# A fused attention, Fourier mixing and MLP kernel: the first chunk is transposed by TensorE, the first Fourier stage goes group by group, attention's first stores stand ahead of the weights' later loads, and the planner's numbers are set anew

## The chip, the cores and the metric

One core of one Trainium2 chip. The metric is the time of one execution in microseconds (us) of device time; lower is better. Engines: PE (TensorE; its weight loads are PEld), DVE (VectorE), ACT (ScalarE), POOL (GpSimd), and SP, which only issues DMAs.

## The reference

```python
q, k, v: (8, 8, 576, 64) float32; w_ch1: (512, 2048) and w_ch2: (2048, 512) float64
attn = softmax(mask(q @ k.T / 8)) @ v    # heads 0 to 3: the last 32 positions; 4 to 7: every 32nd position
x    = attn with its heads side by side                        # (8, 576, 512)
u    = x + real(fft(fft(x, axis=1), axis=2))
un   = (u - mean) / sqrt(var + 1e-6)                           # over the last axis
out  = u + relu(un @ w_ch1) @ w_ch2                            # (8, 576, 512) float32
```

## The kernel before

The work is one stream in which four stages overlap. **Attention** takes a batch b as four pairs of heads (b, hp); its outputs go through DRAM (`xd[b]`). **The Fourier stage** (`fft_batch`) reads `xd[b]` back: `xa` by a DMA on SP, and the mirrored rows `xb` by four indirect DMAs on POOL (`fft_load`, L891 to L899). It forms E = xa + xb and O = xa - xb (L907), folds columns (the steps called cosa to cosf and sin, on DVE, ACT and POOL), multiplies by tables on PE (the product A, five column groups; then B, three row blocks), and `sums` adds x to give u. For batch 0 this is done in float32 (`products32`, L1041), for the others in split float16. **Norm** (L1152) normalises 128 rows of u and brings them to PE's layout: `un` (float32) is split into a high and a low float16 half (ACT L1176, DVE or POOL L1179), and one DMA transpose on SP (L1181) writes the tile `uT`. **The MLP** takes 18 chunks of 256 rows: `ups` (L1387, 8 steps of 24 matmuls into PSUM `ph`), `hidden` (L1403 to L1406) and `downs` (L1427). Chunks from `FC=15` on use a folded (Strassen-like) form with other weights, built late by `folds`.

**Weights** arrive as float64, in 16 pieces of 512 KB for each matrix, and are turned into float32 by integer tricks on ACT and DVE (L1221 to L1237, steps c1, cl, sg, c2). TensorE sums their squares into a Gram matrix (L1264), from which scales follow (L1283 on); then they are split into float16 halves: `split` for the first matrix (L1303, L1306), `scaled` for the second (L1339, L1342, and a DMA L1344). Pieces 0 to 7 of the first matrix load straight into place, pieces 8 to 11 into the tiles that held batch 0's q and k (both L1209), pieces 12 to 15 and all of the second matrix through other buffers (L1215), each from a list of kinds (`S0`, `S1`: `u`, `f6`, `uT`, `kt`, `qk`, `pt`), and only after batch 0's gather has landed (`need="xb0"`). A first-matrix product needs its quarter of the split weights; chunk 0's first `downs` needs the second matrix's. c2 of piece i of the second matrix needs the split of piece i of the first, whose place it takes.

**What sets the order.** The program's text does not: each piece of work is a generator that yields `op(engine, cost, get=buffers, need=events, ...)`, and a planner (`Order.run`) picks, in its own model of time, the next op of each engine: the earliest to start, and among those within a small window (`WS`, `WV`, ...) the one with the lowest `bias`, its urgency. The instructions are then issued in that order on each engine's queue. Most of the dictionary `P` holds such urgencies: `l0` for batch 0's loads, `a0` its attention, `w0a` pieces 0 to 11 of the first matrix, `w0` pieces 12 to 15, `f0` batch 0's Fourier stage, `p0` chunk 0's norm, `t2` the third row block's sums, `w1` the second matrix, `a1`, `an` + `db` per batch the later attention. An op with `alt` goes to whichever engine comes first in the plan, with a handicap from `P` (`LO0`, `LE0` for batch 0's O and E: 12.4 and 13.0). While a Gram bank is open, the planner fills PE's planned gaps with small matmuls that change nothing (`rest`, L1272), which keeps PE's clock up:

```python
n = int((est - self.free["T"] - 0.3) / 0.11)
```

`LQ=0` means that no weight load is issued by ACT. `big` is a room of two PSUM tiles of two banks each; `u` is a room of 8 slots, of which each Fourier batch takes 4.

## Time and profile before

| what | us |
|---|---|
| three runs | 948.23, 951.56, 952.43 (median 951.56) |
| the profiled execution | 948.67 |
| its span | 946.9 |
| PE busy in the span | 910.9 |
| DVE, ACT, POOL busy | 717.0, 506.2, 343.5 |

The profile is that of one execution; its span begins with the first instruction and ends with the last, and the execution's own time is 1.8 us longer. Times in rows are us from the span's start unless marked ns. "Busy" of PE counts the filling matmuls too.

### The profile page before, as it was taken

The page shows a single profiled execution, that of the slowest core. Times are in us where ns is not written, and L with a number is a line of the kernel's source. Part 1 is how long each engine was busy: PE and PEld are TensorE (multiplying, and loading weights), DVE is VectorE, ACT ScalarE, POOL GpSimd, SP SyncE. Part 2 cuts the span into 40 slices and gives each one's busy share as a digit, 9 for nine tenths or more (in the row PEclk, how much of TensorE's full clock was granted, in tenths as well). Part 3 has the DMA queues.
Part 4 walks back from the last instruction along what each step waited for, and adds up shares of the span by engine and source line. Part 5 has one row for each costly group of instructions (what it writes and reads, how often), then busy time and mean ns, then how long its engine had stood idle before and what let it go on. Part 6 is the DMA issues. An engine that isn't in the chain of part 4 may idle for free.

```text
span 946.9 us, 25320 instructions
## 1 busy us (share of the span) xinstructions
PE 910.9 (96%) x10597; PEld 668.4 (71%) x10599; DVE 717.0 (76%) x1342; ACT 506.2 (53%) x987; POOL 343.5 (36%) x315
## 2 busy tenths in 40 slices
PE   8778999999899999999999999999999999999997
PEld 6656885766666667665766677676666766689996
DVE  5988875678783896747956966697679889788675
ACT  4848874554653655643746564646423444365452
POOL 0240332245353631335325522552246256334000
PEclk9969999999999999999999999999999999999999
DMA  9788485363335635584445524625240102021100
GB/s 320 243 327 276 136 217 164 121 174 56 92 89 132 151 81 107 105 156 102 117 88 169 116 86 100 173 73 145 44 125 1 45 7 56 18 52 24 41 24 24
DMA packets 140371, 108.41 MB, mean 114 GB/s; under 512 B 108256, under 2 KB 118752, under 8 KB 140256
## 3 DMA queue, kind: packets, MB, share of 16 engines
q1 hardware_dynamic: 137696, 98.40, 38.7%
q0 software_dynamic: 2560, 8.39, 3.0%
q8 instruction: 83, 1.36, 0.6%
q14 instruction: 32, 0.26, 0.1%
HBM read 64.26 MB, written 18.89 MB: 88 GB/s over the span
## 4 chain that ended last, share of the span: by engine, by line
PE 77%; DMA 8%; DVE 7%; issue 3%; POOL 2%; ACT 2%; SPq 1%; DVEq 0%; POOLq 0%; ACTq 0%
PE acc L1427 28%; PE ph L1387 27%; PE acc L1714 5%; PE f L1571 2%; PE B L1038 2%; DMA xb<-xd,ridx 2%; DMA q<-in_w 2%; PE A L1015 1%; PE s L484 1%; DVE fold L1481 1%; PE o L515 1%; DMA W<-in_w 1%; DMA vn<-in_vl 1%; PE f_0x L1571 1%; DMA q<-in_qk 1%
## 5 line engine op out<-in xcount | busy, mean ns | idle before, releaser
L1387 PE MATMUL ph<-uT,W 128*128 128x256 f16 x2880 | 329.3, 273 | 1.2 <-DMA uT<-hb 1.2
L1387 PEld LDWEIGHTS <-W 128*128 128x128 f16 x2880 | 277.4, 98 | 42.8 <-DMA uT<-hb 1.4
L1427 PE MATMUL acc<-W,hb 128*128 128x512 f16 x1344 | 302.6, 379 | 1.5 <-DVE ub L1437 1.5
L1406 POOL TENSOR_TENSOR hb<-hf,hb 128x512 f16<-128x512 f32 x112 | 160.7, 1435 | 279.0 <-ACT hb L1404 196.5
L1427 PEld LDWEIGHTS <-hb 128*128 128x128 f16 x1344 | 129.2, 98 | 143.8 <-issue 1.7
L1403 ACT ACTIVATE hf<-ph 128x512 f32<-128x512 f32 x120 | 71.2, 593 | 180.7 <-PE ph L1387 113.1
L1404 ACT ACTIVATE hb<-ph 128x512 f16<-128x512 f32 x112 | 66.2, 591 | 0.0
L1481 DVE TENSOR_TENSOR fold<-fold,W 128x512 f32<-128x512 f32 x64 | 52.4, 847 | 0.3
L1714 PEld LDWEIGHTS <-tail 128*128 128x128 f16 x504 | 48.3, 98 | 5.3
L461 DVE SCALAR_TENSOR_TENSOR kt<-qk,sc,kt 128x576 f16<-128x576 f32 (+1 forms) x40 | 37.7, 982 | 3.3 <-ACT kt L446 3.1
L907 POOL TENSOR_TENSOR O<-xa,xb 128x1536 f32<-128x1536 f32 x8 | 33.5, 4189 | 16.0 <-DMA xb<-xd,ridx 12.4
L1161 POOL TENSOR_TENSOR rstd<-mv,negh 128x1 f32<-128x1 f32 x30 | 21.7, 730 | 44.0 <-DVE mv L1158 39.5
L1571 PEld LDWEIGHTS <-tail 128*128 128x128 f16 x576 | 34.7, 98 | 2.6 <-issue 1.4
L1658 POOL TENSOR_TENSOR hb<-hb 128x256 f32<-128x256 f32 x13 | 12.2, 950 | 65.4 <-DVE hb L1658 64.3
L1714 PE MATMUL acc<-fold,tail 128*128 128x256 f16 x288 | 35.0, 273 | 0.0
L446 ACT ACTIVATE kt<-qk,sc 128x576 f16<-128x576 f32 (+1 forms) x40 | 29.3, 784 | 10.1 <-DVE sc L402 9.0
L1140 ACT ACTIVATE pq<-B,fcm 128x128 f32<-128x128 f32 (+7 forms) x105 | 27.3, 380 | 11.5 <-PE B L1038 6.3
L1684 DVE TENSOR_TENSOR tail<-hb,tail 128x512 f16<-128x512 f32 (+1 forms) x47 | 31.8, 704 | 1.9 <-ACT tail L1681 1.5
L1681 ACT CAST tail<-hb 128x512 f16<-128x512 f32 (+1 forms) x48 | 25.6, 563 | 9.1 <-DVE hb L1658 5.5
L1179 DVE TENSOR_TENSOR unp<-un,unp 128x512 f16<-128x512 f32 x28 | 22.6, 806 | 9.1 <-ACT unp L1176 9.1
L1028 DVE SCALAR_TENSOR_TENSOR AT<-A,AT 128x290 f16<-128x290 f32 (+3 forms) x35 | 15.1, 479 | 18.8 <-ACT AT L1023 17.1
L897 POOL DMA_INDIRECT xb<-xd,ridx x24 | 26.7, 1111 | 7.3 <-issue 6.1
(313 smaller groups left out, 1550.9 us busy)
## 6 DMA issues: line engine op xcount, KB each, us to landing
qk<-in_qk SPq DMA_DIRECT2D x28, 592.0 KB
sa<-in_w SPq DMA_DIRECT2D x19, 512.0 KB
out<-ub SPq DMA_DIRECT2D x32, 256.0 KB
vn<-in_vl SPq DMA_DIRECT2D x10, 432.0 KB
W<-in_w SPq DMA_DIRECT2D x8, 512.0 KB
xd<-xo SPq DMA_DIRECT2D x16, 256.0 KB
xa<-xd SPq DMA_DIRECT2D x8, 512.0 KB
vn<-in_vs SPq DMA_DIRECT2D x10, 384.0 KB
```

The lines of the kernel that those rows point to most:

```text
L446: A.activation(hi, src, AF.Copy, scale=f)
L461: V.scalar_tensor_tensor(out=lo, in0=src, scalar=f, in1=hi, op0=ALU.mult, op1=ALU.subtract)
L907: tt_ = lambda e, o, x, y, op: e.tensor_tensor(out=o, in0=x, in1=y, op=op)
L1387: T.matmul(ph[:, i, :], W1[:, 4 * (f0 // 512) + d, x, f0 % 512 : f0 % 512 + 128], self.uhl[y][:, d, :], start=(n == 0), stop=(n == 11))
L1403: A.activation(hf, ph, AF.Relu, scale=HS)
L1404: A.activation(hh, ph, AF.Relu, scale=HS)
L1406: G.tensor_tensor(out=hl, in0=hf, in1=hh, op=ALU.subtract)
L1427: T.matmul(self.acc[s], (hh, hl)[x][:, i, 128 * s : 128 * s + 128], W2[:, f, 1 - y, :], start=(f == 0 and n == 0), stop=(f == 15 and n == 2))
L1481: on(e).tensor_tensor(out=w, in0=w if x is None else x, in1=y, op=ALU.add if f else ALU.subtract)
L1571: T.matmul(dst[:, 128 * f : 128 * f + 128], w(x, i)[:, 128 * f : 128 * f + 128], u(y, i), start=opens and f == 0 and n == 0, stop=closes a ...
L1684: on(o).tensor_tensor(out=lo, in0=src, in1=hi, op=ALU.subtract)
L1714: T.matmul(dst, hop[:, x, j, 128 * i : 128 * i + 128], w(y, i), start=bank not in opened, stop=q == 3 and z in (6, 5, 3, 4) and i == 1 and ...
```

## The change

Five edits. (1) In `norm`, chunk 0 alone is transposed by four float32 TensorE transposes of `un` into a `big` tile, and ACT and DVE then write the two float16 halves from PSUM straight into `uT`; the DMA transpose is left out for it. (2) In `products32`, each of the five groups of A is an op of its own with its own copy from PSUM, and the first row block of B is cut in two: its first part needs only the first three groups. (3) In `att_first`, each pair's stores are a thread of their own with urgency -40. (4) First-matrix pieces from `OW=8` on are loaded only after the events of all four pairs' stores. (5) Numbers: `E` and `O` of batch 0 get the handicaps -26.3 and -2.9; `w0a` becomes lower than `a0`; the list `S1` uses `u` slots (two per piece) for five pieces in place of one, `uT` for one in place of four, and `kt` for two in place of four; `M1=(0, 10)` turns two pairs of second-matrix pieces into double ones; the rest are small shifts. `LQ` stays 0. The diff, cut:

```diff
@@ -20,16 +20,16 @@
 B, H, S, D = 8, 8, 576, 64
 
 P = dict(
-    SL2=2.667, SLD2=1.764, GL0=2.7, GD=7.0, LAT=2.22, GL=3.1, t2=47.947, l0=-31.68, a0=-20, sq0=-23.456, w0a=-19.97,
-    c=12.731, z=13.906, f0=-24.028, w0=-22.847, s0=-1.359, w1=3.314, s1=-5.983, p0=-26.912, p1=4.962, pn=-4.352,
-    a1=-14.294, f1=-1.92, a2=0.121, f2=8.514, an=8.61, fn=-44.611, db=1.982, up=19.467, dn=25.786, ev=0.684, WS=0.271,
-    WV=0.084, WA=0.048, WG=0.877, WT=0.185, SL=0.0, SLD=0.818, np=3, AL=3.136, SG=2.918, Lcl=-0.367, Lsg=0.875, LQ=0,
-    LO0=12.439, LE0=13.019, Lc20=-1.501, LSD0=-13.8, al=0.0, Lfs=-1.909, Lwl=-2.741, Lul=-9.275, LO=24.795, LE=5.158,
-    Lc2=-1.062, LSD=-13.902, Lsub=1.259, Lsub0=28.179, Lrt=14.582, Lu=5.511, ORD0=(3, 2, 0, 1),
+    SL2=2.667, SLD2=1.764, GL0=2.7, GD=7.0, LAT=2.22, GL=3.1, t2=32.862, l0=-31.68, a0=-20, sq0=-23.456, w0a=-27.697,
+    c=9.163, z=-19.15, f0=-17.605, w0=-24.7, s0=-1.676, w1=3.484, s1=-7.438, p0=-23.68, p1=4.962, pn=-5.318, a1=-14.294,
+    f1=-1.761, a2=0.709, f2=8.514, an=8.61, fn=-44.611, db=2.56, up=19.467, dn=25.786, ev=1.736, WS=0.048, WV=0.084,
+    WA=0.048, WG=0.932, WT=0.185, SL=0.0, SLD=0.818, np=3, AL=3.136, SG=2.918, Lcl=-0.367, Lsg=0.875, LQ=0, LO0=-2.864,
+    LE0=-26.259, Lc20=-1.677, LSD0=-14.257, al=-0.345, Lfs=-1.909, Lwl=-2.733, Lul=-22.823, LO=19.663, LE=5.158,
+    Lc2=-0.996, LSD=-13.902, Lsub=0.551, Lsub0=22.353, Lrt=13.061, Lu=5.511, OW=8, ORD0=(3, 2, 0, 1),
     vo=([], [], [], [0, 1, 2, 3]), S0=('qk', 'qk', 'kt', 'pt'),
-    S1=('uT', 'kt', 'f6', 'uT', 'kt', 'uT', 'f6', 'f6', 'kt', 'pt', 'uT', 'qk', 'u', 'f6', 'kt', 'qk'), M1=(), HB=4,
-    RB=1, UB=8, VS=1, FC=15, tp=-0.006, ts=0.377, fq=-18.063, fh=-13.401, ff=-23.53, pf=5.385, Lfold=79.934, Lus=0.177,
-    Lhl=1.519,
+    S1=('u', 'u', 'f6', 'uT', 'u', 'f6', 'f6', 'f6', 'kt', 'pt', 'u', 'u', 'qk', 'f6', 'kt', 'qk'), M1=(0, 10), HB=4,
+    RB=1, UB=8, VS=1, FC=15, tp=-0.406, ts=0.309, fq=-18.063, fh=-13.174, ff=-23.53, pf=11.989, Lfold=80.705, Lus=0.177,
+    Lhl=1.525,
 )
 ORD0 = P["ORD0"]
 FP32 = {(b, hp) for b in range(3) for hp in range(4)}
@@ -777,6 +777,9 @@
             yield op("V", 1.35 if hp < 2 else 1.5, put="acc" if acc else "big", note=f"out {hp}")
             g = att_out(0, hp, po, 1e-9, None, xos[hp])
             next(g)
+            spawn(stored(hp, g), bias=-40)
+
+        def stored(hp, g):
             yield op("S", 0.8 if hp < 2 else 1.6, n=3 if hp < 2 else 6, sets=f"xd0_{hp}", note=f"xd0 {hp}")
             next(g, None)
 
@@ -1046,13 +1049,14 @@
         last = ta[0:33, 4 * NE : 6 * NE], tb[0:33, 767 : 767 + 2 * NE]
         for gs in ((0, 1), (2,), (3, 4)):
             first, end = gs[0] == 0, gs[-1] == 4
-            yield op("T", 1.4 * len(gs), get="big f6 -fft" if first else "acc" if len(gs) == 1 else "big", need=f"FH{257 if end else 0 if first else 129}_{b} f32 second",
-                     put="f6 f6 f6" if end else "", note=f"A{gs[0]} {b}")
-            if first:
-                AT = f6(f"AT{b}")[:, 0 : 10 * NE].rearrange("p (g k) -> p g k", g=5)
-                ATs = AT.rearrange("p g (k t) -> p g t k", t=2)
-            ps = (psone if len(gs) == 1 else lambda b, n: psbig(n))(b, f"A{b}_{gs[0]}")
             for i, g in enumerate(gs):
+                yield op("T", 2.2, get="" if i else "big f6 -fft" if first else "acc" if len(gs) == 1 else "big", need="" if i else f"FH{257 if end else 0 if first else 129}_{b} f32 second",
+                         put="f6 f6 f6" if end and i else "", note=f"A{g} {b}")
+                if first and i == 0:
+                    AT = f6(f"AT{b}")[:, 0 : 10 * NE].rearrange("p (g k) -> p g k", g=5)
+                    ATs = AT.rearrange("p g (k t) -> p g t k", t=2)
+                if i == 0:
+                    ps = (psone if len(gs) == 1 else lambda b, n: psbig(n))(b, f"A{b}_{gs[0]}")
                 c0, w = GROUPS[g]
                 cs = 0 if g < 3 else 1
                 d0 = 0 if g < 2 else 129 if g == 2 else 257
@@ -1062,8 +1066,7 @@
                     o = ps[0:w, 512 * i + NE * t : 512 * i + NE * t + NE]
                     T.matmul(o, sd[:, t, d0 : d0 + w], ta[:, 2 * NE * cs + NE * t : 2 * NE * cs + NE * t + NE], start=False, stop=(t == 1))
 
-            def evac(gs=gs, ps=ps):
-                for i, g in enumerate(gs):
+                def evac(g=g, i=i, ps=ps, gs=gs):
                     w = GROUPS[g][1]
                     o = op("A", 0.4, put=("acc" if len(gs) == 1 else "big") if i == len(gs) - 1 else "", sets=f"AT{g}_{b}", note=f"AT{g} {b}", alt=dict(V=(0.48, P["LAT"])))
                     yield o
@@ -1073,11 +1076,11 @@
                     else:
                         V.tensor_copy(ATs[0:w, g], src)
 
-            spawn(evac())
+                spawn(evac())
         cols = (0, 257, 4), (2, 256, 4), (1, 256, 2), (2, 256, 2), (1, 256, 2)
         for t in range(3):
             r = 128 if t < 2 else 33
-            yield op("T", 2.74, get="big" + (" u u" if t < 2 else ""), need=" ".join(f"AT{g}_{b}" for g in range(5)), put="f6" if t == 2 else "", note=f"B{t} {b}")
+            yield op("T", 2.74 if t else 1.64, get="big" + (" u u" if t < 2 else ""), need=" ".join(f"AT{g}_{b}" for g in range(5 if t else 3)), put="f6" if t == 2 else "", note=f"B{t} {b}")
             ps = psbig(f"B{b}_{t}")
 
             T.matmul(ps[:, 0:512], zerb, zero.to_broadcast([128, 512]), start=True, stop=False)
@@ -1085,6 +1088,8 @@
             for g, (c0, w) in enumerate(GROUPS):
                 x = AT[0:w, g, 128 * t : 128 * t + r]
                 k0, k1, st = cols[g]
+                if t == 0 and g == 3:
+                    yield op("T", 1.1, need=f"AT3_{b} AT4_{b}", note=f"Bb {b}")
                 if g == 0:
                     T.matmul(ps[0:r, 0:257:4], x, tb[0:w, 0:65], start=False, stop=False)
                     T.matmul(ps[0:r, 260:509:4], x, tb[0:w, 1:64], start=False, stop=False)
@@ -1167,6 +1172,18 @@
         else:
             un = mp.tile([128, 2, 257], F32, tag=tag, name=f"un{nm}", bufs=P["RB"] if tag == "rt" else 1).rearrange("p a b -> p (a b)")[:, 0:DM]
         V.tensor_scalar(un, u, mv[:, 0:1], rstd, op0=ALU.subtract, op1=ALU.mult)
+        if c == 0:
+            yield op("T", 0.6, get="big", put=tag, note=f"uturn {nm}")
+            ps = psbig(f"ut{nm}")[:, 0:DM]
+            for d in range(4):
+                T.transpose(ps[:, 128 * d : 128 * d + 128], un[:, 128 * d : 128 * d + 128], ident)
+            yield op("A", 0.62, note=f"uhi {nm}")
+            ps = ps.rearrange("p (d t) -> p d t", t=128)
+            hi, lo = (uT[:, 4 * x : 4 * x + 4, 128 * s : 128 * s + 128] for x in range(2))
+            A.copy(hi, ps)
+            yield op("V", 0.75, put="big", sets=f"uT{nm}", note=f"ulo {nm}")
+            V.tensor_tensor(out=lo, in0=ps, in1=hi, op=ALU.subtract)
+            return
         yield op("A", 0.62, get=ptag, note=f"uhi {nm}")
         if ptag == "h":
             hs = hfree.pop(0)
@@ -1203,7 +1220,7 @@
             src = list(wpieces(wi))[i + n][0]
             if kind is None:
                 far = i + n < P["LQ"]
-                yield op("A" if far else "S", 0.4 if far else 1.45, dma=1.25 if far else 0.0, lat=1.6, need=f"sc{ORD0[(i - 8) // 2]}" if i >= 8 else "", at=0 if n else None, note=f"ld {wi} {i + n}")
+                yield op("A" if far else "S", 0.4 if far else 1.45, dma=1.25 if far else 0.0, lat=1.6, need=(f"sc{ORD0[(i - 8) // 2]}" if i >= 8 else "") + ("".join(f" xd0_{hp}" for hp in range(4)) if i >= P["OW"] else ""), at=0 if n else None, note=f"ld {wi} {i + n}")
                 if n == 0:
                     stg = stg1(i, m)
                 (nc.scalar if far else nc.sync).dma_start(stg[:, 512 * n : 512 * n + 512], src)
```

## Rows read from the trace of the kernel before

**Rows 1.** The page's part 1: busy us of each engine, share of the span, instructions

```profile
PE 910.9 (96%) x10597; PEld 668.4 (71%) x10599; DVE 717.0 (76%) x1342; ACT 506.2 (53%) x987; POOL 343.5 (36%) x315
```

**Rows 2.** Three stretches: length; busy us of PE, PEld, DVE, ACT, POOL; clock; DMA

```profile
0.00:92.30 92.30, 72.29 (x1028) 57.05 (x1030) 73.11 (x134) 56.94 (x73) 19.00 (x19) 0.87 0.86 292
92.30:136.00 43.70, 43.02 (x601) 37.64 (x602) 36.46 (x80) 36.34 (x54) 13.94 (x12) 1.00 0.61 165
136.00:946.90 810.90, 795.63 (x8970) 573.76 (x8968) 607.39 (x1130) 412.92 (x861) 310.55 (x285) 1.00 0.36 92
```

**Rows 3.** The filling matmuls (line 1272), sum of stretches from 0 to 200 us

```profile
sum 200.00, PE 26.32 PEld 24.59; mean PE 1.32 PEld 1.23
```

**Rows 4.** The chain that ended last: start, us, what held it

```profile
37.98 1.97 DMA xd<-xo
...
45.95 3.89 DMA xb<-xd,ridx
...
87.97 4.31 DMA uT<-hb
```

**Rows 5.** Timeline: start, us, instruction; batch 0's stores and what stands among them

```profile
21.89 7.26 SPq L859 DMA_DIRECT2D xd<-xo  x6
...
29.13 0.76 DVE L842 TENSOR_TENSOR xo<-o,rs 128x576 f32<-128x576 f32 x1
...
29.46 1.58 SPq L1209 DMA_DIRECT2D q<-in_w  x2
...
37.43 1.15 SPq L847 DMA_DIRECT2D xd<-xo  x2
```

**Rows 6.** Timeline: E, O and folds of batch 0

```profile
50.05 1.76 DVE L907 TENSOR_TENSOR E<-xa,xb 128x1536 f32<-128x1536 f32 x1 [1.08 <-DMA xb<-xd,ridx]
50.09 5.00 POOL L907 TENSOR_TENSOR O<-xa,xb 128x1536 f32<-128x1536 f32 x1 [2.75 <-DMA xb<-xd,ridx]
...
51.85 4.05 DVE L907 TENSOR_TENSOR tmp<-E 128x765 f32<-128x765 f32 x1
...
57.21 0.95 DVE L907 TENSOR_TENSOR E<-O 128x765 f32<-128x765 f32 x1
```

**Rows 7.** Line 907's O on POOL, all batches: ns min/median/max, first and last start

```profile
L907 POOL TENSOR_TENSOR O<-xa,xb x8: 3442/4142/5029, 50.1 to 710.3; 128x1536 f32<-128x1536 f32 x8
```

**Rows 8.** PE in stretches of 2 us: busy, granted clock, DMA share, GB/s

```profile
54.00:56.00 2.00, 0.00 (x0) 0.50 0.97 375
...
72.00:74.00 2.00, 2.00 (x51) 0.50 0.23 94
```

**Rows 9.** Timeline: the end of A, its last copy, and the start of B

```profile
68.57 1.33 PE L1063 MATMUL A<-f32a,O 128*128 128x145 f32 x4
...
71.40 0.51 ACT L1072 COPY AT<-A 128x290 f32<-128x290 f32 x1
...
73.97 0.55 PE L1083 MATMUL B<-zero 128*128 128x512 bf16 x1
```

**Rows 10.** Timeline: six earlier TensorE transposes, and chunk 0's second norm

```profile
13.98 0.88 PE L760 MATMUL pT<-ident,pbt 128*128 128x128 f32 x6
...
84.86 0.55 DVE L1169 TENSOR_SCALAR un<-ub,mv,rstd 128x512 f32<-128x512 f32 x1 [0.45 <-POOL rstd L1161]
...
85.44 0.62 ACT L1176 CAST hb<-un 128x512 f16<-128x512 f32 x1 [0.28 <-DVE un L1169]
...
87.26 0.68 DVE L1179 TENSOR_TENSOR hb<-un,hb 128x512 f16<-128x512 f32 x1
```

**Rows 11.** The later weights' loads (ns, first and last start), and chunk 0's first `downs`

```profile
L1215 SPq DMA_DIRECT2D sa<-in_w x19: 327/369/1005, 52.8 to 112.1; - x19
...
136.01 1.46 PE L1427 MATMUL acc<-W,h 128*128 128x512 f16 x6
```

**Rows 12.** The stretch of batch 0's gather and first folds: columns as in rows 2

```profile
46.00:59.00 13.00, 7.34 (x106) 6.08 (x103) 11.64 (x11) 2.29 (x6) 7.90 (x4) 0.80 0.72 236
```

**Rows 13.** Timeline of PE: its longest wait after 100 us, in brackets

```profile
249.23 0.38 PE L1015 MATMUL A<-csin,FH 128*127 128x145 f16 x3 [2.69 <-DVE AT L1028]
```

More of the change, by code (lines that the diff above doesn't have):

```diff
@@ L709, in loads @@
             for i, hp in enumerate(ORD0):
-                yield op("S", 1.5 if i else 2.7, sets=f"q{hp}", at=0, note=f"q {hp}")
+                yield op("S", 1.75 if i else 2.0, sets=f"q{hp}", at=0, note=f"q {hp}")
                 nc.sync.dma_start(q0s[hp][:, 0 : S + KP], a["qk"][0, hp])
@@ L723, in loads @@
                 for z in [ORD0[n] for n in P["vo"][i]]:
-                    yield op("S", 1.25 if z < 2 else 1.0, at=0, sets=f"v{z}", note=f"v {z}")
+                    yield op("S", 1.65, at=0, sets=f"v{z}", note=f"v {z}")
                     nc.sync.dma_start(src0[z], a[f"v0{z}"])
```

## The prediction

> **What bounds the kernel now.** I read the page's first part, then stretches, then the chain that ended last, then the timeline where the chain leaves PE. PE is busy 910.9 of 946.9 us [rows 1], but that alone misleads: it counts matmuls that only fill gaps. So I cut the span where the nature of the work changes [rows 2]. From 136.0 on PE is busy 795.6 of 810.9 us at full clock; the 15.3 us left are the last stores after PE's end and small waits, the longest of them 2.69 us [rows 13]. That stretch is bound by PE's own work, which the change leaves as it is. Between 92.3 and 136.0 PE is busy 43.0 of 43.7 us, but DVE and ACT too stand at 83%: they prepare the second matrix while PE works off chunk 0's eight `ups`, four of chunk 1 (there are four `hb` buffers) and batch 1's attention. Before 92.3 PE idles 20.0 us, and of its 72.3 busy us 26.3 are fill [rows 2, 3]; from 54 to 74 its clock is granted at 0.50, that is 1.2 GHz, after a stretch without a matmul [rows 8]. So nearly all that can be won lies ahead of chunk 0's first `ups` at 92.3, and it counts only as far as PE has real work afterwards.
>
> The chain of the head [rows 4] is: batch 0's last store lands at 39.95; the gather's last piece lands at 49.84; E, folds and A; B; sums and norm; the DMA transpose lands at 92.28; `ups`. A second chain hangs on the same gather: the later weights may load only then, from 52.8 on [rows 11], and chunk 0's first `downs` waits for them until 136.0.
>
> **The change part by part.** *Stores first.* Pair 1's output is ready at 29.13 + 0.76 = 29.89, yet its last store is issued at 37.43 to 38.58: SP first spends 7.26 us on six stores of pair 3 and then issues loads of weights [rows 5]. With every store at -40 and pieces 8 to 11 behind them, three issues after 29.89 end near 31.5, if the earlier pairs' stores are out by then, which the -40 asks for. That is 38.58 - 31.5 = 7 us. It moves two things. The first weight loads now stand behind stores that SP must wait for, so pieces 1 to 7 land later; and pieces 8 to 11 (2 MB) stand ahead of `xa` in SP's queue. At the 375 GB/s of a full stretch [rows 8] 2.1 MB take 5.6 us. The gather takes 49.84 - 37.43 = 12.4 us from the last issue on, mostly POOL's own issues, so those loads fit beside it; I take 1 us off, with bounds 0 and 5.6; the other way, 2 us more are won if the weights that DVE works on ahead of pair 1's output come too late to hold it up. ACT is busy 2.29 of the 13 us from 46 to 59 [rows 12]: that is the cover for the weights' later arithmetic. Without it, they'd hold chunk 0's fifth `ups`, not its first. Gather: **-6** (-9 to -1).
>
> *E to POOL, O to DVE.* The handicaps decide it: 3.45 - 26.3 beats 1.78 for E, 1.78 - 2.9 beats 3.45 for O. Before, DVE's E took 1.76, POOL's O 5.00, and the next fold 4.05, where a fold of that shape takes 0.95 [rows 6]; that fold ended at 55.90, 0.81 after O ended. So one engine held the other up; E, then O's 5.00 - 1.72 = 3.3, then the fold's last 0.8 came in series. If the other order is in series too, the fold that needs E ends after 1.76 + 3.3 + 0.95 = 6.0 us, against 5.85 before. If they don't hold each other up, it ends after POOL's 3.44 to 4.14 [rows 7] and 0.95, 4.4 to 5.1. I take **0**, bounds -1.5 and +0.4, nearest to the rows of this very place. The Trainium skill's page "SBUF — State Buffer", section "Who interferes with whom", says that GpSimd's port pair is DVE's second one and that the loser blocks for the whole instruction; by it the first reading holds and this swap, which puts the tensor needed first on the slower engine, wins nothing. By the medians alone it would have won 0.7 us; both lie in the bounds.
>
> *A and B by groups.* Five groups of A end at 68.57 + 1.33 = 69.90; the last copy ends at 71.91; B starts at 73.97, as Gram and score matmuls were put between [rows 9]. B's first part now needs only three groups, copied long before, and can start at 69.90. The copies of groups 3 and 4 run beside it. Lower bound 0 (other matmuls still go first: the weights' `w0` is now lower than `f0`), upper 4.1; **-3**, near the upper end because no wait is left there. B's matmuls are as many as before; the five separate ops add no instruction.
>
> *The transpose.* From `un`'s end at 85.41 to `ups` at 92.3 is 6.9 us: ACT 0.62, DVE 0.68 after other DVE work, then the DMA's 4.31 [rows 4, 10]. The new way: four transposes at 0.88/6 = 0.15 make 0.6, then ACT 0.62, DVE 0.68 (both read PSUM now; I take the same), and some 0.4 for hand-overs: 2.3. **-4.6** (-5.0 to -2.5, if a `big` tile is late: B's third block holds one of two until its sums). The two DMA transposes also leave SP's queue, where weight loads stood behind them. PE's cost is 1.2 us for both halves, where it idles or fills.
>
> *Other buffers and double pieces.* Two pieces in one go cost less than two alone; by the planner's own costs (0.69 twice against 1.15 for c1, 1.35 twice against 2.5 for sg, 0.7 twice against 1.24 for c2) both pairs together save 1.2 us of ACT and DVE, which I count as nothing of its own. Five pieces in `u` slots instead of one can hold up B when they are late: B's first two blocks need four of the eight slots. *All loads on SP* removes nothing: `LQ` is 0 in both.
>
> **Sum.** Chunk 0's `ups` start 6 + 0 + 3 + 4.6 = 13.6 us earlier, near 79. But PE's 43.0 us of work then have to last until the first `downs`. The second matrix's loads wait for the gather, so they come 6 us earlier, and I give freed queue, buffers and ACT's idle time 2 us more: `downs` at 128. The other 5.6 us of the 13.6 become fill or idle on PE. So **8 us** are left: 948.7 - 8 = 940.7 for an execution like the profiled one; that one lies 2.9 below the median of the runs, so the median goes from 951.6 to **943.5**. What is late next is the second matrix.
>
> **Rivals.** (a) *The second matrix keeps up*: then the whole 13.6 counts, 938. For it: DVE's 4.05 contains 3 us of waiting, and ACT is idle near the gather [rows 6, 12]. Against: DVE at 83% after [rows 2]. (b) *The second matrix does not move*: DVE and ACT have the same sum of work, pieces 1 to 11 arrive later and collide with the folds; then all of it becomes fill, and 0 to 3 us remain: 950. For it: the same 83%. Against: the loads' start is tied to the gather. That `LQ` makes one part of the change empty belongs here: it gives 0. (c) *Slower, by the later urgencies*: `db` spaces the later batches wider (1.98 to 2.56) and the folded chunks' norm is less urgent (5.4 to 12.0). A chunk whose u is late leaves PE dry, as at 249 for 2.69 us [rows 13]. There are six later batches with such a place; if each costs 2.5 us more, 15 are lost, 7 more than won: 958. It decides above 8/6 = 1.3 us a batch. Against: PE idles only 15.3 us in 811 there now, the end included [rows 2], so the old spacing has slack to give.
>
> **How the numbers follow.** Forecast 0.45, (a) 0.17, (b) 0.20, (c) 0.18. A measurement of this kernel tells some 0.5%, 4.8 us, from no change. Forecast and (a) lie below 946.8: faster 0.62; (b) within: same 0.20; (c) beyond 956.3: slower 0.18. Forecast and (a), with the gather's bounds and some 4 us of other waits after 136, reach down to 934; (b) and half of (c) reach up to 956.
>
> **What would show it.** Right: the last `xd` store of batch 0 issued near 31 to 33, the gather landed at 42 to 46, E on POOL, B's zeroing matmul within 2 us of A's end, no DMA transpose before the first `ups`, that one at 77 to 82, and the first `downs` at 126 to 130 with fill or idle before it. Wrong: a gather past 47 (SP blocked behind loads), `ups` waiting on a `big` tile or a `u` slot, `downs` still at 136, or PE's idle after 136 above 20 us.

## The result, and the profile after

The changed kernel is slower by 1%: a median of 958.60 us over 7 runs (955.73 to 962.64), against 950.87 over 7 runs (946.57 to 952.43) of the kernel before; the ratio is 1.0098, with an interval of 1.0074 to 1.0122. The forecast was 8 us faster, and the time lies above its range. The profiled execution took 958.1 us with a span of 956.2, 9.3 more than before.

The page's first part, then the three stretches of [rows 2] with the last one's end moved:

```profile
PE 917.3 (96%) x10623; PEld 674.8 (71%) x10623; DVE 713.0 (75%) x1333; ACT 506.1 (53%) x986; POOL 343.6 (36%) x317
```

```profile
0.00:92.30 92.30, 69.01 (x858) 54.85 (x859) 63.57 (x114) 50.43 (x61) 23.87 (x19) 0.82 0.77 270
92.30:136.00 43.70, 41.26 (x645) 35.22 (x642) 40.09 (x81) 36.28 (x53) 11.74 (x11) 1.00 0.48 143
136.00:956.20 820.20, 806.99 (x9126) 584.74 (x9124) 609.33 (x1139) 419.38 (x874) 307.96 (x287) 1.00 0.37 93
```

Past 136 PE idles 13.2 us, less than the 15.3 of before: the later batches lost nothing. In the first 92.3 us PE's idle time grows from 20.0 to 23.3, DVE does 63.6 us of work instead of 73.1 and ACT 50.4 instead of 56.9 [rows 2]. The head has grown, and it is the two engines of the weights' arithmetic that did less in it. Windows of ten us say when (columns as in rows 2); first the kernel before, then the changed one:

```profile
20.00:30.00 10.00, 8.00 (x147) 7.12 (x148) 8.23 (x13) 8.19 (x9) 0.00 (x0) 1.00 0.98 383
30.00:40.00 10.00, 6.90 (x89) 6.03 (x87) 9.60 (x21) 9.67 (x9) 0.00 (x0) 0.84 0.77 214
```

```profile
20.00:30.00 10.00, 8.84 (x148) 8.05 (x149) 4.71 (x9) 5.47 (x6) 0.00 (x0) 0.83 0.73 202
30.00:40.00 10.00, 5.16 (x84) 4.58 (x81) 4.74 (x12) 4.57 (x4) 4.33 (x4) 1.00 0.84 284
```

From 20 to 40 DVE works 17.8 us before and 9.5 after, ACT 17.9 and 10.0. Some 8 us of arithmetic of each are pushed behind 40, where the folds of batch 0 want the same engines. SP's timeline shows why (start, us, instruction; rows left out are marked), as against [rows 5]:

```profile
15.47 7.87 SPq L862 DMA_DIRECT2D xd<-xo  x12
23.38 0.84 SPq L1226 DMA_DIRECT2D W<-in_w  x2
...
28.26 1.16 SPq L850 DMA_DIRECT2D xd<-xo  x2
29.46 2.85 SPq L1226 DMA_DIRECT2D W<-in_w  x4
32.41 2.46 SPq L1226 DMA_DIRECT2D q<-in_w  x4
34.97 0.40 SPq L896 DMA_DIRECT2D xa<-xd  x1
45.06 0.33 SPq L390 DMA_DIRECT2D f32a<-in_f32a  x1
```

The last store goes out at 28.3 to 29.4, 9 us earlier than in [rows 5]; 7 were forecast. The gather's last piece `xb` has landed by 45.06 (the last row waits for it), 4.8 us earlier than before. But ten of the twelve early weight pieces now stand behind stores that SP has to wait for, and eight of them (4 MB) ahead of `xa`. What that does to the pieces is seen on the engines' timelines. The kernel before (the last of these pieces reaches ACT; the third scale of the first matrix on PE, L359; the last of its split on DVE; the start of A, and of `ups`):

```profile
35.66 1.22 ACT L1221 ACTIVATE q<-q 128x1024 f32<-128x1024 f32 x1 [0.30 <-DMA q<-in_w]
43.68 0.16 PE L359 MATMUL gram<-s1w,oneb 128*128 128x1 bf16 x1 [0.72 <-DVE s1w L1285]
45.25 3.73 DVE L1306 SCALAR_TENSOR_TENSOR W<-W,scl,W 128x1024 f16<-128x1024 f32 x3
57.13 1.20 PE L1060 MATMUL A<-f32a,FD 33*65 33x290 f32 x2 [5.45 <-DVE FD L907]
92.32 8.03 PE L1387 MATMUL ph<-uT,W 128*128 128x256 f16 x72 [1.21 <-DMA uT<-hb]
```

The changed kernel, with E, O and the first fold of batch 0, which [rows 6] show for before (`tmp`, and its last step into `FD`), the start of A, a wait inside it, and `ups`:

```profile
47.96 1.17 ACT L1238 ACTIVATE q<-q 128x1024 f32<-128x1024 f32 x1 [1.74 <-DMA q<-in_w]
49.29 4.52 POOL L910 TENSOR_TENSOR E<-xa,xb 128x1536 f32<-128x1536 f32 x1 [10.62 <-ACT q L1238]
51.56 7.70 DVE L1254 SCALAR_TENSOR_TENSOR W<-q 128x1024 int32<-128x1024 int32 x2 [0.56 <-ACT q L1248]
53.77 4.41 POOL L910 TENSOR_TENSOR O<-xa,xb 128x1536 f32<-128x1536 f32 x1
59.19 0.94 DVE L910 TENSOR_TENSOR tmp<-E 128x765 f32<-128x765 f32 x1
60.89 0.16 PE L359 MATMUL gram<-s1w,oneb 128*128 128x1 bf16 x1 [0.50 <-DVE s1w L1302]
61.13 2.78 PE L1289 MATMUL gram<-oneb,zero 128*128 128x128 bf16 x47
61.72 0.62 DVE L910 TENSOR_TENSOR FD<-tmp 128x192 f32<-128x192 f32 x2
63.84 0.70 PE L1064 MATMUL A<-f32a,FD 33*65 33x290 f32 x2
66.25 6.21 DVE L1323 SCALAR_TENSOR_TENSOR W<-W,scl,W 128x1024 f16<-128x1024 f32 x4
70.04 0.85 PE L1067 MATMUL A<-f32a,E 128*128 128x145 f32 x2 [2.59 <-POOL E L910]
102.67 2.78 PE L1404 MATMUL ph<-uT,W 128*128 128x256 f16 x24
```

The last pair of pieces reaches ACT 12.3 us later and the third scale comes 17.2 us later. Before, all of this work was over at 48.98, 1.1 us before E could start; now it lies among the folds: on DVE the last c2 (L1254) stands ahead of the fold, and the split (L1323) between the folds and A's later groups; on PE the Gram matmuls, the scale and 47 fill matmuls stand ahead of A. A starts 6.7 us later: its first folds are ready at 62.34 instead of 57.30, which is 5.0 of them, and then PE works off the fill until 63.84. E waited for `xa`: its row names ACT's q, but that ended at 49.13, and the load on SP that waits for `xa` to land starts at 49.14. Chunk 0's `ups` start at 102.67, 10.35 later than before (92.32).

### The profile page after: what moved, and what is told of

It reads as the page before. It is cut to its first block, busy times and chain, and to the rows that moved or that the text cites. A ratio compares the mean times of both kernels' runs of the same rounds, so it can differ in the third digit from the quotient of the medians.

```text
span 956.2 us, 25370 instructions
## 1 busy us (share of the span) xinstructions
PE 917.3 (96%) x10623; PEld 674.8 (71%) x10623; DVE 713.0 (75%) x1333; ACT 506.1 (53%) x986; POOL 343.6 (36%) x317
## 4 chain that ended last, share of the span: by engine, by line
PE 80%; DVE 7%; DMA 7%; ACT 3%; issue 2%; SPq 1%; POOL 0%; DVEq 0%; ACTq 0%; POOLq 0%
PE ph L1404 30%; PE acc L1444 29%; PE acc L1731 6%; PE f L1588 3%; PE B L1041 2%; DVE W L1254 2%; DMA W<-in_w 1%; PE A L1018 1%; DMA q<-in_w 1%; PE s L484 1%; PE o L515 1%; PE f_0x L1588 1%; DMA q<-in_qk 1%; PE f_2x L1588 1%; DMA pT<-qk 1%
## 5 line engine op out<-in xcount | busy, mean ns | idle before, releaser
L1423 POOL TENSOR_TENSOR hb<-hf,hb 128x512 f16<-128x512 f32 x112 | 156.7, 1399 | 282.1 <-ACT hb L1421 189.5
L1498 DVE TENSOR_TENSOR fold<-fold,W 128x512 f32<-128x512 f32 x64 | 55.7, 899 | 0.3
L910 POOL TENSOR_TENSOR O<-xa,xb 128x1536 f32<-128x1536 f32 x8 | 33.5, 4186 | 4.8 <-DMA xb<-xd,ridx 4.8
L1675 POOL TENSOR_TENSOR hb<-hb 128x256 f32<-128x256 f32 x12 | 10.5, 882 | 58.3 <-DVE hb L1675 57.1
L1289 PEld LDWEIGHTS <-zero 128*128 128x128 bf16 x386 | 27.9, 112 | 4.7 <-issue 4.0
L1289 PE MATMUL gram<-oneb,zero 128*128 128x128 bf16 x386 | 30.0, 245 | 0.0
```

The costliest lines, as they stand in the source:

```text
L910: tt_ = lambda e, o, x, y, op: e.tensor_tensor(out=o, in0=x, in1=y, op=op)
L1289: T.matmul(idle[-1][:, 0:128], zerb, oneb, start=False, stop=False)
L1423: G.tensor_tensor(out=hl, in0=hf, in1=hh, op=ALU.subtract)
L1498: on(e).tensor_tensor(out=w, in0=w if x is None else x, in1=y, op=ALU.add if f else ALU.subtract)
```

## The experiments

One table for all (us, read from the timeline of one execution each; idle + fill is PE's in the first 100 us; the ratio is to the kernel before, with its interval). Differences of 2 us between two timelines mean little: x12 has the plan of the kernel before and other instructions only in `norm`, and yet its scale and A come 1.8 us later.

| kernel | third scale | A | B | `ups` | first `downs` | idle + fill | ratio |
|---|---|---|---|---|---|---|---|
| before | 43.7 | 57.1 | 74.0 | 92.3 | 136.0 | 46.3 | 1 |
| changed | 60.9 | 63.8 | 80.0 | 102.7 | 134.4 | 54.7 | 1.0098 |
| x1 E, O swapped | 62.7 | 66.8 | 85.1 | 108.1 | 147.0 | 55.4 | 1.0092 (1.0058 to 1.0126) |
| x2 no -40 | 58.2 | 64.8 | 81.2 | 106.0 | 160.7 | 50.1 | 1.0362 (1.0325 to 1.0399) |
| x3 DMA transpose | 60.1 | 63.6 | 79.2 | 104.0 | 144.5 | 55.1 | 1.0171 (1.0127 to 1.0215) |
| x4 before, TensorE transpose | 45.6 | 59.0 | 75.0 | 93.3 | 139.0 | 46.6 | 1.0013 (0.9997 to 1.0030) |
| x5 `xa` ahead, planned anew | 69.3 | 94.6 | 110.1 | 131.9 | 147.4 | 69.3 | 1.0336 (1.0310 to 1.0363) |
| x6 old numbers | 69.7 | 87.0 | 97.5 | 116.6 | 143.3 | 63.9 | 1.0157 (1.0129 to 1.0185) |
| x7 before, groups | 44.7 | 58.2 | 70.7 | 94.1 | 144.7 | 46.6 | 1.0229 (1.0198 to 1.0259) |
| x8 before, groups, `ph` | 45.5 | 59.0 | 71.5 | 95.3 | 148.2 | 45.1 | 1.0208 (1.0175 to 1.0241) |
| x9 held, `xa` ahead | 63.5 | 66.4 | 82.6 | 105.3 | 136.9 | 55.5 | 1.0143 (1.0102 to 1.0183) |
| x10 held, and E on DVE | 60.3 | 63.2 | 79.4 | 104.2 | 135.9 | 52.1 | 1.0134 (1.0096 to 1.0173) |
| x11 held, `ph` | 61.8 | 65.8 | 81.0 | 105.3 | 137.1 | 52.3 | 1.0142 (1.0097 to 1.0187) |
| x12 before held, `ph` | 45.5 | 58.9 | 75.6 | 93.2 | 136.9 | 45.9 | 1.0012 (0.9992 to 1.0032) |
| x13 held, pieces by POOL | 68.3 | 71.3 | 87.5 | 110.2 | 141.9 | 56.5 | 1.0191 (1.0168 to 1.0214) |
| x14 x13, E on DVE, `ph` | 66.6 | 69.6 | 85.8 | 110.3 | 141.9 | 54.4 | 1.0181 (1.0153 to 1.0209) |
| x15 held, 4 pieces out | 63.0 | 66.0 | 82.2 | 106.7 | 138.4 | 53.0 | 1.0140 (1.0117 to 1.0163) |
| x16 x6, `f6` after A | 71.6 | 71.8 | 83.8 | 104.5 | 158.6 | 53.8 | 1.0186 (1.0155 to 1.0216) |
| x17 before held, late scale | 60.1 | 69.3 | 84.6 | 102.8 | 146.9 | 56.5 | 1.0102 (1.0069 to 1.0136) |
| x18 x16, A ahead | 68.8 | 58.2 | 76.3 | 103.0 | 158.0 | 50.3 | 1.0198 (1.0144 to 1.0251) |

**Parts undone or done alone, planned anew.** x1 gave E and O their old handicaps, `LO0=12.439, LE0=13.019`:

> The changed kernel with one edit: the handicaps of batch 0's E and O are those of before (LE0=13.019, LO0=12.439), so E goes to DVE and O to POOL again. Theory E (both on POOL in series, 49.29 to 58.18, held the fold back to 59.19): the fold of E ends some 4 us earlier after the gather, near 55.5 instead of 60.13, and chunk 0's first `ups` at about 98 to 99 instead of 102.67; the time falls by about 4 us, to 954 to 955. Rival Q (the head is held by SP's queue and by weights' work alone): the fold ends earlier but `ups` stay at 102 to 103, and the time stays at 957 to 960.

E went back to DVE, but behind the pieces: it started at 59.1, and `ups` came at 108.1, later than either theory had it. Neither way of placing E and O is worth anything here; the time did not move.

x2 put the stores' urgency back: `spawn(stored(hp, g))` without `bias=-40`.

> The changed kernel with one edit: the four pairs' stores keep the urgency of the values (about -19.8) instead of -40, so the first matrix's eight first loads stand ahead of all stores on SP, as before; pieces 8 to 11 still come after the stores. Theory Q (SP waits for the stores' data with six weight loads behind it, and 4 MB then stand ahead of `xa`): only 2 MB stand ahead of `xa`, E starts some 3 to 5 us earlier than 49.29 even if the last store is issued later than 28.8, `ups` start at 98 to 100, the time is 954 to 956. Rival (the stores' early issue is what helps, and the loads behind it cost nothing): the last store goes out near 36, E starts at 50 or later, and the time is 959 to 962.

Neither came: the last store went out at 33.5, E started at 48.3, and it is some 25 us slower than the changed kernel (0.0264 of 950), and much of that lies far behind the edit (`downs` 26 us later, PE idle 8.2 us between 180 and 260 where it was 2.7). The planner had laid out everything differently.

x3 left the TensorE transpose out of the changed kernel, x4 put it alone into the kernel before (both by the block at `if c == 0` in `norm`):

> The changed kernel without its first edit: chunk 0's norm goes through the float16 tile and the DMA transpose again. If the TensorE transposes are worth the forecast's 4.6 us even here, `ups` start near 106 to 107 and the time rises to 962 to 963. If their gain was lost to the wait for a PSUM tile (98.92, released by the subtraction of attention's scores at 98.78), `ups` start at 102 to 104 and the time stays within 2 us of 958.6.

> The kernel before with one part of the change alone: chunk 0 is transposed by TensorE through a `big` tile. The forecast's step: from un's end to the first `ups` 2.3 us instead of 6.9, `ups` near 88 instead of 92.3, and 2 to 4 us off the time (947 to 949), less what the second matrix holds back. Rival (a `big` tile is late here too, since attention's scores and the third block of B hold both): 5 to 7 us from un to `ups`, time within 1 us of 950.9.

x3 is 0.7% slower, but `ups` only 1.3 us later; `downs` came 10 us later in the new plan. x4 gains nothing: `ups` come 7.4 us after `un`'s end.

x5 moved `xa` ahead by numbers, `f0=-28.5, OW=4`; x6 kept the new code and took all of the old numbers, with `OW=8`; x7 put the groups of A and B alone into the kernel before; x8 added the transpose with its tile from `ph`.

> The changed kernel with two numbers set otherwise (f0 from -17.605 to -28.5, OW from 8 to 4), so that on SP the load of xa stands right behind the last batch-0 store, ahead of the last four W pieces and the four q pieces (4 MB); the planner then also puts O on DVE and leaves E on POOL. Theory Q (the gather stood behind 4 MB on SP, and O on POOL cost 4.2 us more): xa is issued near 30 and lands by 40 to 43, E starts there instead of at 49.3, and chunk 0's first ups come at 92 to 95 instead of 102.7; since PE was idle or filling before it, 7 to 9 us come back: 950 to 952. Rival M (the end of the head is set by the second matrix, whose arithmetic follows the order of the loads and not the gather): ups come earlier, but the first downs stay within 2 us of 134 or later, and the time is 956 to 962.

> The code of the changed kernel with every urgency of the kernel before (all of P but OW, and S1, M1, tp, ts, pf, Lfold and the like): stores first, A and B by groups and the TensorE transpose stay, single pieces instead of double ones. SP then has xa behind five W pieces instead of eight W and four q, E is on DVE and O on POOL as before. Theory U (the new urgencies are what costs): 943 to 951, with ups at 84 to 90 and the first downs by 134. Rival S (the new structure itself makes the loads late, as all of them but one stand behind stores on SP): slower than before still, 954 to 962, with the second matrix's first W scaled later than 130 and the first downs past 136.

> The kernel before with A and B by groups alone. SP's queue and the gather stay as they were (E at 50 to 52). Theory H (what comes off the head's chain comes off the time): B starts within 1 us of A's end, 3 to 4 us earlier, un ends at 81 to 82.5, ups come at 88.5 to 89.5, and the time is 947 to 949. Rival M (the second matrix sets the end of the head): ups as early as that, but the first downs at 135 to 138 and the time 950 to 953.

> The kernel before with A and B by groups and the TensorE transpose of chunk 0, which takes its PSUM tile from the ph buffers (idle until the first ups) instead of from the two big ones; urgencies, stores and loads as before. No wait for a big tile is left: from un's end to ups 2.5 to 4 us instead of 6.9. Theory H: ups at 84 to 86, time 943 to 947. Rival M: ups at 84 to 86, the first downs at 135 to 138, the time 949 to 953.

None of the four came within either theory's range of the time, and all are slower than the changed kernel too. x5 and x6 did what was wanted of the gather (E at 46.5 and 45.3) and yet A came at 94.6 and 87.0. x7 shows two things. B does start 3.2 us earlier, but at the lower clock; windows of x7 (third number from the end: the granted clock) have 0.50, that is 1.2 GHz, from 70 to 76, where the kernel before has 0.92 from 74 to 76 and 1.00 then, and B takes 11.2 us (70.73 to 81.97) instead of 8.6:

```profile
74.00:76.00 2.00, 1.78 (x5) 1.09 (x6) 1.12 (x2) 1.38 (x4) 0.00 (x0) 0.50 1.03 412
180.00:260.00 80.00, 73.30 (x878) 51.50 (x876) 58.31 (x115) 44.53 (x102) 29.93 (x37) 0.94 0.42 105
660.00:760.00 100.00, 95.77 (x960) 65.16 (x958) 66.63 (x118) 40.70 (x84) 36.83 (x34) 0.98 0.29 72
760.00:860.00 100.00, 93.93 (x766) 66.19 (x764) 89.11 (x141) 43.09 (x93) 33.89 (x29) 0.95 0.09 24
```

And an edit of batch 0 alone, in the first 100 us, cost PE idle time at 180 to 260 (77.31 busy before) and past 660 (100.00 and 97.34 busy before in the same two windows). So the time of a variant that is planned anew says little about the part that was edited. From here on the plan was held where that is said: the planner sees what it saw, and single instructions are moved or replaced by hand at their places.

**Parts alone, with the plan held.** x9: the DMA of `xa` issued when the fourth pair's stores are out:

```diff
             next(g, None)
+            xa_now.append(hp)
+            if len(xa_now) == 4:
+                xa_now.append(xa_load(0))
```

x10: also E by `V` and O by `G` for batch 0. x11: the transposes in `pph.tile(...)` instead of `psbig(...)`. x12: the kernel before, in `norm` for chunk 0:

```diff
-            A.copy(unp[:, 0], un)
+            for d in range(4):
+                T.transpose(ps[:, 128 * d : 128 * d + 128], un[:, 128 * d : 128 * d + 128], ident)
+            A.copy(hi, ps)
...
-            nc.sync.dma_start_transpose(uT[:, :, 128 * s : 128 * s + 128], unp.rearrange("p x d -> p (x d)"))
```

> The changed kernel with its plan held: the planner sees what it saw, every engine keeps its order, and only the DMA of xa is issued by hand right behind the last batch-0 store, ahead of the four W and four q pieces. Theory Q (xa behind 4 MB held E up): xa lands before the gather, E starts on POOL at about 45 instead of 49.3; DVE has the two q pieces in its order ahead of the fold, and they land 1 to 1.5 us later than now, so the fold tmp comes at 56 to 57 instead of 59.2 and ups at 100 instead of 102.7: 2 to 3 us, 955 to 957. Rival D (DVE's order, not xa, is what the fold waits for): tmp within 1 us of 59, ups within 1 us of 102.7, 958 to 960.

> As x9, and E and O of batch 0 on the engines of the kernel before (E on DVE at the place in DVE's order that the plan gives, O on POOL), again with the plan held. Theory P (O on POOL behind E cost 4.2 us): O on POOL from about 45 to 50, E on DVE at 51 to 53, the fold tmp at 54 to 56, ups at 98 to 99.5; 3 to 5 us less than the changed kernel, 953 to 956. Rival D: E stands behind the weights on DVE and the fold comes at 57 or later; 956 to 959.

> The changed kernel with its plan held, and the two TensorE transposes written to the ph buffers instead of the big ones. Theory B (the second transpose waited for a big tile, and that ate the 4.6 us): from un's end to ups 3.5 to 5 us instead of 7.8, ups at 98 to 100, time 955 to 957. Rival M (what follows ups has slack, as the second matrix sets the first downs): ups as early, the first downs within 1.5 us of 134.4, the time 957 to 960.

> The kernel before with its plan held, chunk 0's DMA transposes replaced at their places by TensorE transposes into the ph buffers. The term of the sum by itself: un's end to ups 2.5 to 3.5 us instead of 6.9, ups at 88 to 89.5. Theory H (the head's chain counts in full): 946 to 948. Rival M (the second matrix is the bound from there on): the first downs at 135 to 137 still, and 949 to 952.

x9: E starts at 45.43, 3.9 us earlier, as theory Q has it, and the fold comes at 60.64, even 1.4 later, beyond rival D's range too; the time is no better (1.0143). The last pair of pieces, now behind `xa`, reaches ACT at 50.92, 3.0 us later, so x9 alone doesn't tell the two apart; x15 below, without the loads of the last two pairs, has the fold at 60.68 still. DVE of x9:

```profile
46.03 4.48 DVE L1331 SCALAR_TENSOR_TENSOR W<-W,scl,W 128x1024 f16<-128x1024 f32 x1
50.43 4.45 DVE L1262 SCALAR_TENSOR_TENSOR W<-W 128x1024 int32<-128x1024 int32 x1
...
58.37 2.35 DVE L1262 SCALAR_TENSOR_TENSOR W<-q 128x1024 int32<-128x1024 int32 x2
60.64 0.95 DVE L918 TENSOR_TENSOR tmp<-E 128x765 f32<-128x765 f32 x1
```

The pieces' instructions fill DVE's queue up to the fold, and while POOL runs E and O (45.4 to 53.8) two of them take 4.5 us each instead of 1.2. x10 wins 3.2 us of A by giving E back to DVE, but 1.1 of `ups` and nothing that the runs can tell; the fold comes at 58.5, as rival D had it. x11 takes the wait for a `big` tile away, and from `un`'s end to `ups` it is still 7.5 us (97.75 to 105.28), against 7.8. x12 shows why the transpose wins nothing even in the kernel before. Its PE after the second transpose, and the DVE instruction that ends `uT`:

```profile
87.67 0.66 PE L1174 MATMUL ut<-ident,un 128*128 128x128 f32 x4 [1.86 <-DVE un L1169]
88.16 2.79 PE L1283 MATMUL gram<-oneb,zero 128*128 128x128 bf16 x47
89.46 0.68 DVE L1179 TENSOR_TENSOR uT<-ut,uT 128x512 f16<-128x512 f32 x1
90.95 0.60 PE L573 MATMUL s<-mloc,ident 128*128 128x480 bf16 x3
91.48 1.04 PE L580 MATMUL s<-qk 64*64 64x96 f32 x36
92.45 0.86 PE L1275 MATMUL gram<-W 128*128 128x128 bf16 x12
93.16 2.02 PE L1398 MATMUL ph<-uT,W 128*128 128x256 f16 x17
```

`uT` is whole at 90.14, 2.5 us after `un`'s end at 87.61, as the forecast's 2.3 had it. But planned fill, the scores of batch 1 and Gram matmuls stand ahead of `ups` in PE's order, and `ups` start at 93.16; scores and Gram matmuls ran under the DMA before. The fill, 2.8 us, stays only because the plan is held; what `ups` would win without it is not shown.

**What holds A.** The table's third scale and A go together: in the changed kernel and its variants but x5, x6 and x18, A follows the scale by 0.1 to 6.6 us, mostly by 3; in the kernel before and its variants, x17 apart, by 13.4. Part of that is the order alone: the 3 us are the 47 fill matmuls that every held plan of the changed kernel has between the two. A stands behind the first phase of the weights on PE, and its folds behind it on DVE. x13 gave the loads of pieces 2 to 11 to POOL's queue, `nc.gpsimd.dma_start(...)` at the place of pieces 0 and 1; x14 joined x10 and x11 to it; x15 left out the loads of pieces 8 to 11 (`if i < 8:`) in x9; x16 was x6, planned anew, with `need="xb0 AT0_0" if kind == "f6" else "xb0"` for the second matrix's loads.

> The changed kernel with its plan held; the loads of the first matrix's pieces 2 to 11 (5 MB less the first two pieces) are issued by POOL at the place of pieces 0 and 1, so that none stands behind a store on SP, and xa stands right behind the last store. E and O stay on POOL. Theory W (late weight pieces hold the folds and A, as DVE and PE have them ahead in their order): the third scale's matmul on PE comes at 43 to 50 instead of 60.9, the fold tmp at 50 to 55 instead of 59.2, A at 55 to 59 instead of 63.8, ups at 94 to 98 instead of 102.7; 949 to 954. Rival P (POOL's E and O alone hold DVE until they end, whatever the pieces do): tmp at 55 or later, A at 60 or later, 955 to 958.

> As x13, with E of batch 0 on DVE and O on POOL, and chunk 0's transposes in the ph buffers; plan held. Theory W: E at 44 to 47, tmp ends by 52, A at 52 to 56, ups at 90 to 94, and as PE has work until the first downs near 130 to 134 the time is 944 to 950. Rival M (the second matrix is then the bound): ups as early, the first downs at 133 to 136 with more fill or idle before it, 950 to 955.

> As x9 (plan held, xa right behind the last store), and the loads of pieces 8 to 11 (2 MB) are left out; their arithmetic runs on what lies in the buffers, so the weights are not those of the reference, and two small memsets on POOL fill the buffers' ends. Theory W: without waiting for these loads DVE gets to the fold tmp at 52 to 56 instead of 60.6 in x9, A at 57 to 60 instead of 66.4, ups at 96 to 100, 952 to 957. Rival P: tmp stays at 58 or later, since POOL's E and O (45 to 54) hold DVE up with the pieces' last instructions.

> As x6 (the new code, the old urgencies, planned anew), and the pieces of the second matrix that are staged in an f6 buffer may be loaded only once the first group of A is copied out. Theory F (in x6 the load of piece 2 took the f6 buffer that the last fold freed, and A's copies had to wait until that piece was worked off): A at 60 to 66 instead of 87.0, ups at 93 to 99 instead of 116.6, the time 955 to 961 instead of 964.6. Rival (A waited for the Gram matmuls of the weights): A still past 80.

x13 and x14 missed: the transfers crowded each other. From x13's chain and its ACT (the first row is a weight piece that SP issued at 14.77, after the ten that POOL had issued):

```profile
14.77 19.30 DMA W<-in_w
34.15 1.17 ACT L1244 ACTIVATE W<-W 128x1024 f32<-128x1024 f32 x1 [8.88 <-DMA W<-in_w]
35.23 0.24 ACT L762 COPY pt<-pU 96x128 f32<-96x128 f32 x1
```

The piece landed after 19.30 us; in the changed kernel's chain the same load takes 8.91. ACT waited for it, and a copy that attention's last output needed stood behind it on ACT. So the last store was issued at 38.94, and the third scale came at 68.3. The pieces were not earlier this way, so theory W was not tested.

x15 missed too: DVE still gets the first of pieces 4 to 7 at 39.55, and then POOL's E and O stretch DVE's part of the work as in x9, so the third scale stayed at 63.0. x16 says where 15 us of x6's wait went: with `f6` kept for A, A came at 71.8 and not at 87.0, so in x6's plan a weight piece had most likely held A's buffer. A and the time (1.0186) still missed theory F's ranges. It is also the clearest case of the queue: its fold of E ended at 53.1, the last fold into `FD` on DVE at 60.4, and POOL's parts at 65.0, yet A stood behind the weights (PE):

```profile
69.62 1.03 PE L1281 MATMUL gram<-W 128*128 128x128 bf16 x8 [0.55 <-DVE W L1254]
71.64 0.19 PE L359 MATMUL gram<-s1w,oneb 128*128 128x1 bf16 x1
71.76 1.23 PE L1064 MATMUL A<-f32a,FD 33*65 33x290 f32 x2
```

x17 turned it round: the kernel before, its plan, loads, stores and gather untouched, with one ACT instruction of pieces 10 and 11 repeated. x18, planned anew, let A's first groups go without the event `second` in x16.

```diff
-            A.activation(stg.bitcast(F16).rearrange("p (n t) -> p n t", t=4)[:, :, 1], wh.bitcast(F32), AF.Copy)
+            for _ in range(7 if wi == 0 and i == 10 else 1):
+                A.activation(stg.bitcast(F16).rearrange("p (n t) -> p n t", t=4)[:, :, 1], wh.bitcast(F32), AF.Copy)
```

> The kernel before with its plan held, and one suspected cost added by itself: the ACT instruction that puts the sign of pieces 10 and 11 in place (2.49 us) is done seven times instead of once, which moves the third scale by 15 us, from 43.7 to about 58.6, as late as in the changed kernel; loads, stores and the gather stay. Theory W: the rest of the pieces' arithmetic falls among the folds and A's start follows the third scale: A at 60 to 66 instead of 57.1, ups at 96 to 101 instead of 92.3, and the time 953 to 959. Rival S (A's start has slack for it, and what the changed kernel loses comes from elsewhere): A within 1.5 us of 57.1, ups within 2 us of 92.3, 949 to 952.

> As x16, and the first two groups of A need no longer wait for the whole first phase, so that the planner may put them ahead of the last Gram matmuls and the third scale on PE. Theory W: A at 57 to 63 instead of 71.8, before the third scale and not after it, and ups 2 to 8 us earlier than x16's 104.5; the time 958 to 966 instead of 968.3. Rival (the f32 folds, not the pieces, hold A): A at 68 or later.

x17 on ACT, POOL, DVE and PE:

```profile
39.33 17.56 ACT L1232 ACTIVATE q<-q 128x1024 f16<-128x1024 f32 x7
49.99 3.46 POOL L907 TENSOR_TENSOR O<-xa,xb 128x1536 f32<-128x1536 f32 x1 [3.02 <-DMA xb<-xd,ridx]
56.92 1.22 DVE L1238 SCALAR_TENSOR_TENSOR W<-q 128x1024 int32<-128x1024 int32 x1 [15.11 <-ACT q L1232]
60.13 0.18 PE L359 MATMUL gram<-s1w,oneb 128*128 128x1 bf16 x1
65.33 1.75 DVE L907 TENSOR_TENSOR E<-xa,xb 128x1536 f32<-128x1536 f32 x1
69.31 0.70 PE L1060 MATMUL A<-f32a,FD 33*65 33x290 f32 x2
```

With the third scale as late as in the changed kernel, `ups` come at 102.81 (102.67 there) and the ratio is 1.0102 (1.0098 there); A, `ups` and the time lie even beyond theory W's ranges. The delay of that work alone is enough for a loss as large as the whole. What it delays first is DVE's queue: DVE idles 15.11 us for a c2, and E, behind it, starts at 65.33 although the gather was there before 50. x17 is no copy of the changed kernel: ACT works 15 us more, POOL doesn't run E, the first `downs` come at 146.9 and not at 134.4, so that the two times are so nearly equal may be chance. x18 brought A ahead of the scale (58.2), as forecast, but `ups` only 1.5 us and no time: the rest of A, B (granted clock 0.50 from 76 to 84) and the norm then stood among the same work. Past A's start, how much of the loss goes by PE's queue and how much by DVE's was not separated. That taking the delay away gives the loss back is not shown either: no variant of the changed kernel got the third scale earlier than 58.2, and none came out that beats the kernel before; x4 and x12 equal it.

## Why the prediction was wrong

*Stores first: right at the store, wrong behind it.* "Gather: **-6**" got 9 us at the last store and 0.8 at E (49.29 against 50.05). First, `xa` was taken for an issue that fits beside the gather; it landed 4 us after it, behind 4 MB. But x9 and x15 show that an earlier E alone brings no earlier fold. The step that failed is the cover: "Without it, they'd hold chunk 0's fifth `ups`, not its first." ACT's free 13 us at the gather [rows 12] hid nothing, since the work that was to use them stands ahead of the folds on DVE and ahead of A on PE, and each engine did its work in the order of its queue (x17's DVE idled 15.11 us for a c2, the last 6.9 of them with E's data there). The slack to be read was DVE's: 48.98 to 50.05, 1.1 us. Of a delay of 12.3 us in the loads, 17.2 in the third scale, 10.35 came out at `ups`, where 13.6 less were forecast. The prediction asked what waits for these weights, not what is queued behind them.

*E to POOL, O to DVE: **0**.* The plan put both on POOL: 8.9 us in series, with two c2 on DVE stretched to 7.70. The handicap of O was read against costs on idle engines, not against DVE's queue. The bounds (-1.5 and +0.4) missed this: the fold that needs E ends 10.8 us after E's start (60.13), against 5.85 before. Held apart (x10 against x9) it is 3.2 us of A, and no measurable time.

*A and B by groups: **-3**.* B's start came as forecast, right at A's last group (80.03 in the changed kernel, and 3.2 us earlier in x7), and was given back: in x7 by B at the lower clock, in the changed kernel by A, which took 16.4 us (63.84 to 80.24) instead of 12.8: PE waited 3.1 us for POOL's parts of E, which ran beside the split on DVE, and Gram matmuls stood between its groups.

*The transpose: **-4.6**.* The DMA's 4.31 us were counted as a wait. The wait that it ended on PE was 1.21 us (the row at 92.32 above); much of the rest was under scores and Gram matmuls that PE had to do first. x12 and x11 show it without any late tile: x12's `uT` is as quick as forecast, and PE comes to it late. The late `big` tile that the prediction named did come in the changed kernel (the second transpose at 98.92), and taking it away changed nothing.

*Sum and rivals.* `ups` at 102.67 instead of 79, `downs` at 134.39 instead of 128. The second matrix came 1.6 us earlier, which is within what two timelines differ by, and the loss is in PE's idle time and fill of the first 100 us (46.3 to 54.7) and in its clock there (0.88 to 0.83). Rival (b) named what happened ("pieces 1 to 11 arrive later and collide with the folds"), but let it cost the gain at most; `ups` came 10.35 us later than before. Rival (c), 958, has the right time by luck, for a wrong reason: PE's idle time past 136 fell. Of "what would show it wrong", SP blocked behind loads was close: it was the loads that were blocked behind the stores.

## What to carry to other kernels

When a step is moved ahead in a queue, follow what is now behind it to the engine where that work will fall, and look for the slack there, in the order of that engine's queue: an idle engine elsewhere is no cover. A DMA on the chain is worth the idle time that its landing ends, not its own length. In a kernel whose order is planned by costs, test a part with the plan held; planned anew, single edits cost up to 25 us here (x2 against the changed kernel), some of it hundreds of us behind the edit (x7).

## What the runs showed of the hardware

DVE and POOL hold each other up in more than E and O. While POOL ran its E and O over 128x1536 float32, two of DVE's 128x1024 instructions took 4.48 and 4.45 us (x9) instead of 1.2, and two took 7.70 in the changed kernel where two take 2.35 in x9 with POOL at rest. In x17, with DVE idle, O took 3.46 instead of the 5.00 of [rows 6], and the fold of E 0.95 instead of 4.05. The Trainium skill's page "SBUF — State Buffer", section "Who interferes with whom", says that the loser blocks for the whole instruction; the trace agrees (x9's two end at 50.51 and 54.88, each 1.1 us, about its own length, after POOL's E and O end at 49.42 and 53.80), and here it fell on the weights, not only on the folds. Loads that POOL issued held up what SP issued behind them: in x13 a piece issued by SP at 14.77 landed after 19.30 us, so a second queue was no way past the transfers already under way.
